# An attention block with a gated Mish branch on one core: two kinds of VectorE step may be planned onto GpSimd, and the planner's thresholds are set anew

## The chip, the cores and the metric

The kernel runs on one core of a Trainium2 chip. A core has engines with instruction streams of their own: TensorE (PE) multiplies matrices into PSUM, ScalarE (ACT) applies functions, VectorE (DVE) and GpSimd (POOL) do elementwise work, and SyncE (SP) issues most transfers. Engines wait for one another through semaphores. The metric is the device time of one execution in microseconds; the median of three runs of the kernel before is 791.36 us (791.05 to 792.82).

## The reference, cut to what matters

`x` has 2,048 tokens of 640 features. A gate per token mixes multi-head attention (32 heads of 20 features) with a dense layer under Mish.

```python
x = A_x
g = _sigmoid((x * gate_w).sum(-1, keepdims=True))
# a: softmax attention
qkv = (x @ wqkv).reshape(B, S, 3, H, Dh)...          # H = 32, Dh = 20
p = softmax(einsum("bhqd,bhkd->bhqk", q, k) * Dh ** -0.5)
a = einsum("bhqk,bhkd->bhqd", p, v)... @ wo
# b: h = x @ w1 + b1 (1,536 wide); Mish: h * tanh(softplus(h)); then @ w2
b = einsum("bsf,fd->bsd", h * jnp.tanh(sp), w2)
return g * a + (1 - g) * b
```

All inputs and the output are bfloat16.

## The kernel before, in words

**Tiles and steps.** Queries are cut into four blocks `c` of 512, keys into 16 tiles `kt` of 128, and the 32 heads into eight groups `g` of four. A score tile (128 keys by 512 queries of one head) fills one PSUM bank. There are 4 x 8 x 16 x 4 = 2,048 of them, taken three at a time: 683 steps. `emit_s` issues a step's score matmuls (L1197) two steps ahead into banks 0 to 2 or 3 to 5, and `emit_e` the exponential (L1219) from there into a ring ETS of six. `emit_pv` and `pv` multiply the exponentials with V (L1456) into bank 6, for four heads at once. V has a column of ones in front of each head, so the sums of the softmax arise beside the products.

**VectorE's share of the exponentials.** In some steps ScalarE takes two tiles and VectorE the third. `choose` decides on that, step by step. `emit_x` evicts such a tile with a scale and a bias to int16 (L1264), so that its bits read as a rough power of two. When four tiles of a group are together, `close` lists three SBUF steps for them: `fraction` (L1328), `times_y` (L1332) and `power` (L1336). Their results enter the product with V as two terms.

**After a group** of four heads and 512 queries, `group_done` copies bank 6 to OUNG (L1538). A transfer brings the sums to RR, `invert` takes reciprocals (L1545) and sends them to DRAM (L1546), four transfers spread them to BCT (L1552), and `times` (L1506) multiplies OUNG by BCT into the normalised tile. The last group of the last block is cut in two halves of 256 queries; these are turned by VectorE itself (L1523 to L1531), the first half through OUNG.

**The dense branch.** `h_task` computes h, and VectorE adds the bias (L953). For every four 128-row pieces ScalarE makes a tanh (L976) into U, and `mish` lists eight VectorE steps: the first rounds U to half precision (L998, from float32), the others are a polynomial (L998, L1001) and the product with h (L1001). `b_task` multiplies with W2 (L1017, evicted at L1024), `p_task` projects the heads and mixes with the gate (L1041, L1047); `part_task` does the same early for the last block, without the last two groups.

**What sets the order.** A planner in Python writes all five instruction streams out when the kernel is built. `Plan.add` keeps a planned clock for each engine from costs such as WIDE (0.60 us) and TAIL. VectorE's listed SBUF steps wait in lanes: `norm` (reciprocals and products), `soon` (the chains of `close`), `blend` (Mish) and `bg`. The function `dve` puts an eviction on VectorE after `work` has filled the time before it with listed steps that fit. TensorE's other matmuls are tasks with due steps, and `pick`, `put` and the main loop place them into bank 7 (`FB`). `choose` refuses a tile when VectorE owes too much (`BEHIND`, `IDLE`), when a group's chain would end late (`tight`, with `CROWD`), or when tasks lag (`LAG`, `room`). GpSimd has the opening's fills and copies and one addition at the very end (L1864).

Of the kernel before, what the change touches and what calls it, by code (L numbers as in the profile page):

```python
# [37 lines left out]
OLD = 3  # L38
WAITED = 3
OWE = 0.2  # L40
# [15 lines left out]
STREAM = 0.5  # L56
# [3 lines left out]
QUICK = 0.335  # L60
FAST = 0.335
# [18 lines left out]
AHEAD = 14  # L80
SPREAD = 3
GAP = 0.3
SLOW_LOAD = 5.0
# [5 lines left out]
CROWD = 1.4  # L89
MARGIN = 2.5  # L90
EAGER = 20
# [5 lines left out]
SHIFT = 0.2  # L97
LAG = 5
SPARE = 7
WINDOW = 3.41  # L100
CALM = 3
# [4 lines left out]
SQ = 24  # L106
SQ_STEP = 16
H_AT = 150
H_STEP = 12.5
# [3 lines left out]
CUTS = ((0, 256), (256, 256))  # L113
# [17 lines left out]
WARM = 7  # L131
MORE = 8
# [11 lines left out]
class Plan:  # L144
# [3 lines left out]
    def __init__(self, prefix):  # L148
        self.prefix = prefix
        self.ops = []  # L150
        self.now = {e: 0.0 for e in ENGINES}
        self.kind = None
        self.passes = deque()
        self.queue = 0.0

    def add(self, eng, fn, deps=(), slot=None, cost=0.1, kind="F", tail=None, bulk=0.0):
# [12 lines left out]
        if eng == "pe":  # L169
            self.passes.append((at + cost, cost))  # L170
        op.t1 = at + cost + (tail or (TAIL["sp"] if slot else TAIL[eng]))
# [71 lines left out]
def bass_gated_mix__softmax_full_mha__dense_activation_mish__prompt_kernel(  # L243
# [142 lines left out]
    def attention(pl, fast):  # L386
# [10 lines left out]
        now = {"step": -1, "open": None, "bank": False, "rate": 9.0}  # L397
# [45 lines left out]
        def dve(fn, deps=(), cost=0.1, kind="F"):  # L443
# [3 lines left out]
            return pl.add("dve", fn, deps, cost=cost, kind=kind)  # L447
# [5 lines left out]
        def work(until):  # L453
            while True:
                best = None
                lined = sorted([lane for lane in (*soon, blend) if lane], key=lambda lane: lane[0][3])
                for rank, todo in enumerate((norm, *lined, bg)):
                    if todo:
# [7 lines left out]
                        halve = len(todo[0]) > 4 and begin + cost > until  # L466
# [53 lines left out]
        if fast:  # L520
# [114 lines left out]
            def fetch(k, g, c, names):  # L635
# [14 lines left out]
                for dst, src in pairs:  # L650
                    op = pl.add("sp", lambda e, dst=dst, src=src: e.dma_start(dst, src), deps, slot, cost=0.5, bulk=1.3 if k else 0.1)  # L651
# [319 lines left out]
            def mish(ev, hb, hc, k):  # L971
# [9 lines left out]
                def piece(cost, fn, after=None):  # L981
                    def run():
                        last[0] = pl.add("dve", fn, [last[0]], cost=cost)
                        if after:
                            after(last[0])
                    blend.append((cost, run, lambda: last[0], due))
# [16 lines left out]
                piece(WIDE, scalar(W, U, 1.0), read)  # L1003
                piece(QUICK, scalar(B, W, MISH_IN))
                piece(WIDE, times(B, W, B))
                piece(QUICK, scalar(B, B, MISH_MID))
                piece(WIDE, times(B, B, B))
                piece(QUICK, scalar(B, B, MISH_BY, MISH_BY * MISH_OUT))
# [264 lines left out]
        def dve_by(fn, deps, cost, slack):  # L1273
# [3 lines left out]
            return pl.add("dve", fn, deps, cost=cost)  # L1277

        def close(batch):
# [15 lines left out]
            def piece(cost, fns, deps, after=None, split=False):  # L1295

                def run(some, each, mark):
                    def go():
                        for sp in some:
                            op = pl.add("dve", fns(sp), deps(), cost=each)  # L1300
# [696 lines left out]
```

## Time and profile before

| | before |
|---|---|
| median of three runs | 791.36 us |
| profiled execution | 791.27 us |
| its span, first to last instruction | 789.4 us |
| busy, ScalarE | 773.3 us (98%) |
| busy, VectorE | 748.6 us (95%) |
| busy, TensorE | 709.7 us (90%) |
| busy, GpSimd | 20.2 us (3%) |
| exponentials on three tiles / on two | 281 / 402 |

A row of the groups gives line, engine, operation, output<-input with shapes, count, busy time and mean duration of one in ns, and the idle time ahead of it with what ended it. Instructions of one engine overlap by a little, so the distance from one start to the next is shorter than a duration. A row of waits reads: who waited for whom, us in total, times, longest. A row of a timeline begins with the start from the span's beginning and the duration, both in us.

### The profile page before, as it was taken

The page shows a single profiled execution, that of the slowest core. Times are in us where ns is not written, and L with a number is a line of the kernel's source. Part 1 is how long each engine was busy: PE and PEld are TensorE (multiplying, and loading weights), DVE is VectorE, ACT ScalarE, POOL GpSimd, SP SyncE. Part 2 cuts the span into 40 slices and gives each one's busy share as a digit, 9 for nine tenths or more (in the row PEclk, how much of TensorE's full clock was granted, in tenths as well). Part 3 has the DMA queues.
Part 4 walks back from the last instruction along what each step waited for, and adds up shares of the span by engine and source line. Part 5 has one row for each costly group of instructions (what it writes and reads, how often), then busy time and mean ns, then how long its engine had stood idle before and what let it go on. Part 6 is the DMA issues. An engine that isn't in the chain of part 4 may idle for free.

```text
span 789.4 us, 16424 instructions
## 1 busy us (share of the span) xinstructions
PE 709.7 (90%) x6649; PEld 262.4 (33%) x6690; DVE 748.6 (95%) x1313; ACT 773.3 (98%) x715; POOL 20.2 (3%) x21
## 2 busy tenths in 40 slices
PE   8899999889888888999999889999889899999985
PEld 4333333233323332233323233333333333333332
DVE  5899999999999999999999999999999999999995
ACT  6999999999999999999999999999999999999995
POOL 8100000000000000000000000000000000000000
PEclk9999999999999999999999999999999999999998
DMA  8221310212233221402112131202121213000101
GB/s 201 63 59 55 102 52 17 81 55 60 72 91 109 83 64 45 133 17 65 32 29 51 52 90 36 64 19 61 31 85 49 82 48 85 15 28 24 29 15 39
DMA packets 77799, 47.12 MB, mean 60 GB/s; under 512 B 23916, under 2 KB 73700, under 8 KB 77668
## 3 DMA queue, kind: packets, MB, share of 16 engines
q1 hardware_dynamic: 77316, 45.80, 21.0%
q8 instruction: 56, 0.92, 0.5%
q14 instruction: 27, 0.22, 0.1%
q10 hardware_dynamic: 288, 0.16, 0.1%
q0 software_dynamic: 112, 0.01, 0.1%
HBM read 36.26 MB, written 7.52 MB: 55 GB/s over the span
## 4 chain that ended last, share of the span: by engine, by line
ACT 90%; DVE 4%; PE 4%; DMA 1%; issue 0%; SPq 0%
ACT ETS L1219 87%; ACT REG L976 2%; PE PS L1197 1%; PE PS L1456 1%; ACT W2R L976 1%; DVE KT L1332 1%; DVE KT L1264 1%; DMA QT<-QS 1%; PE PS L555 0%; DVE QT L1264 0%; PE PS L1041 0%; SPq L651 0%; PE PS L738 0%; DVE HB L1047 0%; DVE HB L1264 0%
## 5 line engine op out<-in xcount | busy, mean ns | idle before, releaser
L1219 ACT ACTIVATE ETS<-PS 128x1024 bf16<-128x1024 f32 (+1 forms) x683 | 753.9, 1370 | 2.8 <-PE PS L1197 2.8
L1197 PE MATMUL PS<-QT,KT 32*128 32x512 bf16 (+1 forms) x2116 | 267.8, 378 | 57.1 <-ACT ETS L1219 48.1
L1456 PE MATMUL PS<-ETS,V_all 128*21 128x512 bf16 (+1 forms) x1699 | 161.7, 375 | 0.0
L1197 PEld LDWEIGHTS PS<-QT,KT 32*128 32x128 bf16 x2116 | 67.0, 91 | 281.6 <-ACT ETS L1219 255.9
L1264 DVE TENSOR_SCALAR PADS<-PS 128x512 int16<-128x512 f32 x97 | 66.0, 682 | 7.8 <-PE PS L1197 7.3
L1264 DVE TENSOR_SCALAR QT<-PS 128x512 int16<-128x512 f32 x102 | 69.5, 683 | 4.0 <-PE PS L1197 3.4
L1017 PE MATMUL PS<-W2R,HB 128*128 128x320 bf16 x384 | 68.5, 302 | 0.7 <-DVE HB L953 0.5
L1264 DVE TENSOR_SCALAR OTN<-PS 128x512 int16<-128x512 f32 x84 | 57.1, 681 | 0.6 <-PE PS L1197 0.5
L943 PE MATMUL PS<-XB,REG 128*128 128x256 bf16 x360 | 53.6, 274 | 2.3 <-DVE OUTT L1047 1.4
L1456 PEld LDWEIGHTS PS<-ETS,V_all 128*21 128x21 bf16 x1699 | 41.8, 90 | 41.4 <-issue 27.0
L1001 DVE TENSOR_TENSOR U<-U 128x1024 f16<-128x1024 f16 x72 | 49.0, 681 | 0.3
L1017 PEld LDWEIGHTS PS<-W2R,HB 128*128 128x128 bf16 x384 | 30.7, 97 | 32.4 <-issue 19.7
L943 PEld LDWEIGHTS PS<-XB,REG 128*128 128x128 bf16 x360 | 29.1, 97 | 25.8 <-issue 23.5
L953 DVE TENSOR_TENSOR HB<-PS,B1T 128x512 bf16<-128x512 f32 x48 | 32.7, 680 | 0.5 <-PE PS L943 0.3
L998 DVE TENSOR_SCALAR U<-U 128x1024 f16<-128x1024 f16 x72 | 29.9, 415 | 0.5
L1041 PE MATMUL PS<-WOQ,QT 128*128 128x320 bf16 x128 | 24.5, 302 | 2.3 <-DVE HB L1047 0.6
L1264 DVE TENSOR_SCALAR REG<-PS 128x512 int16<-128x512 f32 x38 | 25.7, 682 | 0.2
L1735 PE MATMUL PS<-KT 128*128 128x512 bf16 x79 | 24.1, 383 | 1.7 <-issue 1.1
L1041 PE MATMUL PS<-WOQ,OTN 128*128 128x320 bf16 x128 | 23.8, 302 | 0.2 <-issue 0.2
L815 PE MATMUL PS<-REG,XB 128*128 128x160 bf16 (+1 forms) x240 | 23.1, 234 | 0.0
L976 ACT ACTIVATE REG<-HB 128x1024 f32<-128x1024 bf16 x18 | 22.2, 1236 | 0.0
L660 PE MATMUL PS<-XB,REG 128*128 128x512 bf16 x69 | 20.3, 382 | 1.8 <-issue 1.1
(188 smaller groups left out, 816.0 us busy)
## 6 DMA issues: line engine op xcount, KB each, us to landing
REG<-in_B_w_dram SPq DMA_DIRECT2D x36, 320.0 KB, 3.2
BCT<-SUMS SPq DMA_DIRECT2D x124, 64.0 KB, 2.2
W2R<-in_B_w_dram SPq DMA_DIRECT2D x12, 320.0 KB, 3.8
KT<-KS SPq DMA_DIRECT2D x28, 128.0 KB
QT<-QS SPq DMA_DIRECT2D x112, 20.0 KB
QS<-WOQ SPq DMA_DIRECT2D x16, 128.0 KB, 1.7
KS<-OTN SPq DMA_DIRECT2D x16, 128.0 KB, 1.7
W2R<-in_B_w_dram SPq DMA_DIRECT2D x1, 1920.0 KB, 10.2
```

The lines of the kernel that those rows point to most:

```text
L943: return lambda e, bank: e.matmul(PS[:, bank, i * HW:(i + 1) * HW], w1b(n1)[:, f, i * P:(i + 1) * P], xt(c)[:, f, cols], start=(f == 0), s ...
L953: ev = dve(lambda e: e.tensor_tensor(hb, PS[:, bank, :].rearrange("p (i t) -> p i t", i=2), bias, ALU.add), [last, b_load, *guarded, *b_re ...
L976: ex = pl.add("act", lambda e: e.activation(U, h, AF.Tanh, scale=0.5, bias=-MISH_AT), [ev, u_free[0]], cost=0.95)
L998: return lambda e: e.tensor_scalar(dst, src, *ops)
L1001: return lambda e: e.tensor_tensor(dst, one, two, ALU.mult)
L1017: return lambda e, bank: e.matmul(PS[:, bank, 0:HALF], HB[:, hc % 2, f, t * P:(t + 1) * P], W2[:, f, half * HALF:(half + 1) * HALF], start ...
L1041: return lambda e, bank: e.matmul(PS[:, bank, 0:HALF], otn(c, g, fast)[:, t * P:(t + 1) * P], WOG[:, g, half * HALF:(half + 1) * HALF], st ...
L1197: op = pl.add("pe", lambda e, i=i, g=real(g), tile=tile, j=j, cols=cols, c=c, of_q=of_q: e.matmul(scores(s)[:, i, cols], KT[32 * j:32 * j ...
L1219: e_op[s] = pl.add("act", lambda e: e.activation(ETS[:, s % NETS, 0:n, :], scores(s)[:, 0:n, :], AF.Exp, scale=SCALE, bias=LIFT if fast el ...
L1264: ev = dve_by(lambda e: e.tensor_scalar(block(batch["y"], n, I16), scores(s)[:, 2, :], SCALE * ULPS, BIAS, ALU.mult, ALU.add), [s_op[s], * ...
L1456: lasts[n] = pl.add("pe", lambda e, v=v, j=j, src=src[:, cols], of_q=of_q, count=count: e.matmul(PS[32 * j:32 * j + EW, ACC, of_q], v, src ...
L1735: pl.add("pe", lambda e: e.matmul(PS[:, bank, :], k[:, 0:P], k, start=True, stop=True), [free], cost=PASS, kind="S")
```

## The change

Five things are changed.

- **GpSimd takes steps.** A normalising product and Mish's first step are listed with a job for GpSimd. After each eviction on VectorE, a new function `settle` looks at the row of planned instructions at the end of VectorE's line that are not SBUF steps (these have kind "L"). If the job (1.35 us for a product, 1.05 us for a first step, and 0.1 more) fits beside that row, it goes to GpSimd, behind the instruction that begins the row. `patient` holds such a step back from VectorE for 4 us of VectorE's time after its input is there, except in the last 60 steps. Afterwards either engine may get it.
- **The last two halves** work in U2 in place of OUNG, BCT and RR, and no longer bring the listed products ahead of them.
- **After the last step** tasks take banks 7, 5 and 4 in turn.
- **Order and due steps:** the partial projections are due 36 steps ahead of the end (26 before), the first projections of the last block 12 ahead (2 before); the first queries' pads, the estimate's matmuls and Mish's tasks have other due steps.
- **Thresholds** of `choose` and of the main loop have other values, steps that may move are counted at 0.3 of their cost, and a list NUDGE of 86 values, one for eight steps, is taken from the lateness that `choose` sees.

```diff
-OLD = 3
+OLD = 2
-OWE = 0.2
+OWE = 0.6
-STREAM = 0.5
+STREAM = 0.48
+ASIDE = 1.35
+ASIDE_1 = 1.05
+APART = 0.1
+AWAIT = 4
+SHARE = 0.3
+AWAIT_1 = 0
+CALM_END = 60
-RISK = {"pe": 0.1, "act": 0.3, "dve": 0.5, "pool": 1.2, "sp": 0.6}
-CHAIN = 2.6
+RISK = {"pe": 0.1, "act": 0.3, "dve": 0.5, "pool": 0.3, "sp": 0.6}
+CHAIN = 3.0
-IDLE = 5
+IDLE = 7
-AHEAD = 14
-SPREAD = 3
+AHEAD = 20
+SPREAD = 4
-SLOW_LOAD = 5.0
+SLOW_LOAD = 3.5
-CROWD = 1.4
+CROWD = 1.1
-EAGER = 20
+EAGER = 45
-SHIFT = 0.2
-LAG = 5
+SHIFT = 0.4
+LAG = 25
-CALM = 3
+CALM = 2
-SQ = 24
+SQ = 40
-H_STEP = 12.5
+H_STEP = 14
+DIRECT = 1
+PART_DUE = 36
+LAST_DUE = 12
+FETCH = (2.3, 3.0)
+LEAD = 10
+NUDGE = [-0.5, 0, -0.5, 0, -0.5, 0, 0, 0, -0.5, 0, -0.5, 0, 0, -1, 0.5, 0, 0, 1, 0, 0, -1, -1, 2, 2, 1, 0, 0, 0.5, 0, 0, 0, 0, 2, 3, 0, 0, 0, -1, 0.5, 3, 0, 1, -1, 0.5, 0, 0, 0, 0, 1, 0, 0, 0, 0, 3, 0, -1, 0, 0.5, 1, 1, 2, 2, 2, 3, 0, -1, -0.5, 0, 0, 3, -0.5, -0.5, 3, 0.5, 1, 1, 0, 0.5, 0, 2, -0.5, 0.5, 0.5, 0, 0, 3]
...
+        def settle():
+
+            while fast:
+                for todo in (blend, norm):
+                    job = todo[0][5] if todo and len(todo[0]) > 5 else None
+                    ready = job and job[0]()
+                    if not ready:
+                        continue
+                    line = pl.line
+                    i = len(line)
+                    while i and not line[i - 1][2]:
+                        i -= 1
+                    begin = max(ready.t1 + HOP, pl.now["pool"], line[i - 1][0])
+                    while i < len(line) and line[i][0] <= begin:
+                        i += 1
+                    if begin + job[1] + APART <= pl.now["dve"]:
+                        todo.popleft()
+                        job[2](line[i - 1][1])
+                        break
+                else:
+                    return
+
+        def patient(op, wait):
+
+            return now["step"] < NSLOT - CALM_END and pl.now["dve"] < op.t1 + wait
+
+        def load(job):
+
+            return job[0] * (SHARE if len(job) > 5 else 1)
...
-                piece(WIDE, scalar(W, U, 1.0), read)
+                piece(WIDE, scalar(W, U, 1.0), read, AWAIT)
...
-            late = max(0.0, pl.now["dve"] - pl.now["act"])
-            urgent, other = (sum(t[0] for todo in some for t in todo) for some in ((norm, *soon), (blend, bg)))
+            late = max(0.0, pl.now["dve"] - pl.now["act"]) - NUDGE[s // 8]
+            urgent, other = (sum(load(t) for todo in some for t in todo) for some in ((norm, *soon), (blend, bg)))
...
             if end:
-                while norm:
-                    norm.popleft()[1]()
+                if not fast:
+                    while norm:
+                        norm.popleft()[1]()
...
+                    free = [bc_read[0], rr_read[0], oung_free[0]]
+                    if fast:
+                        bc, rr, free = U2[:, CW:CW + w], U2[:, CW + HW:CW + HW + w // 32], [None] * 3
                     cost = w * COL * 2.6 + 0.09
                     if (c, g) != groups[-1]:
-                        held = OUNG[:, cols]
+                        held = U2[:, 0:w] if fast else OUNG[:, cols]
...
+            if fast and c == NC - 1 and g >= NG - DIRECT:
...
-                norm.append((WIDE, lambda: times(src, wide), lambda: wide[-1]))
+                norm.append((WIDE, lambda: times(src, wide), lambda: False if fast and patient(wide[-1], AWAIT) else wide[-1],
+                             0, None, (lambda: wide[-1], ASIDE, lambda dep: times(src, [*wide, dep], "pool"))))
...
-            parts = [part_task(t, half, NSLOT - 26) for t in range(4) for half in range(2)]
-            parts += [p_task(NC - 1, t, half, NSLOT - 2, True) for t in range(last_t[0]) for half in range(2)]
+            parts = [part_task(t, half, NSLOT - PART_DUE) for t in range(4) for half in range(2)]
+            parts += [p_task(NC - 1, t, half, NSLOT - (LAST_DUE, LAST_DUE, 2)[t], True) for t in range(last_t[0]) for half in range(2)]
...
+        def spot():
+
+            if not fast or now["step"] < NSLOT:
+                return FB
+            bank = (FB, 5, 4)[now["spot"] % 3]
...
```

The branch behind `DIRECT` normalises a group of the last block with VectorE's own transposes in place of transfers.

More of the change, by code (lines that the diff above doesn't have):

```diff
@@ L396, in attention @@
         acts = deque()
-        now = {"step": -1, "open": None, "bank": False, "rate": 9.0}
+        spots = {FB}
+        now = {"step": -1, "spot": 0, "open": None, "bank": False, "rate": 9.0}
         if fast:
@@ L979, in mish, with piece, run @@
                 due = ex.t1 + PATIENCE
-                def piece(cost, fn, after=None):
-                    def run():
-                        last[0] = pl.add("dve", fn, [last[0]], cost=cost)
+                def piece(cost, fn, after=None, wait=0):
+                    def run(eng="dve", *more):
+                        last[0] = pl.add(eng, fn, [last[0], *more], cost=ASIDE_1 if more else cost, kind="L")
                         if after:
                             after(last[0])
-                    blend.append((cost, run, lambda: last[0], due))
+                    dep = lambda: False if wait and patient(last[0], wait) else last[0]
+                    job = (lambda: last[0], ASIDE_1, lambda op: run("pool", op))
+                    blend.append((cost, run, dep, due, None, job) if wait else (cost, run, dep, due))
                 def read(op):
@@ L1369, in tight @@
                 left = ends / TAKEN * EXP
-                before = sum(t[0] for t in blend if t[3] < pl.now["act"] + left)
+                before = sum(load(t) for t in blend if t[3] < pl.now["act"] + left)
                 return (late + urgent + before) * CROWD + need + MARGIN >= left
@@ L1714, in backlog @@
         def backlog():
-            return max(0.0, pl.now["dve"] - pl.now["act"]) + sum(t[0] for todo in (norm, *soon, blend, bg) for t in todo)
+            return max(0.0, pl.now["dve"] - pl.now["act"]) + sum(load(t) for todo in (norm, *soon, blend, bg) for t in todo)
         def pv_ready():
```

68 lines of the change are left out of this document (48 added, 20 removed).

## The prediction

> **What bounds the kernel now.** I read the page's first part, then a table of stages, then ScalarE's waits, then the groups of instructions with shapes kept apart, and last the timeline of VectorE. The stages are: before the first softmax exponential, the first 100 us, the long middle, the last exponentials, and the tail. Behind each engine stand its busy us and, in brackets, its instructions.
>
> ```profile
> span 789.4 us, 16424 instructions
> PE 709.7 (90%) x6649; PEld 262.4 (33%) x6690; DVE 748.6 (95%) x1313; ACT 773.3 (98%) x715; POOL 20.2 (3%) x21
> ```
>
> ```profile
> core 0: us, PE busy (x) PEld busy (x) DVE busy (x) ACT busy (x) POOL busy (x), PEclk, DMA share, GB/s
> 0.00:9.28 9.28, 7.60 (x48) 4.74 (x48) 5.01 (x12) 3.31 (x7) 6.31 (x11) 1.00 0.85 182
> 9.28:100.00 90.72, 81.79 (x878) 32.39 (x887) 78.79 (x138) 89.72 (x83) 13.07 (x10) 1.00 0.32 86
> 100.00:764.00 664.00, 604.32 (x5492) 218.12 (x5518) 649.16 (x1135) 663.22 (x613) 0.00 (x0) 1.00 0.20 55
> 764.00:780.60 16.60, 13.80 (x226) 6.18 (x228) 12.02 (x23) 16.53 (x14) 0.00 (x0) 1.00 0.09 23
> 780.60:789.40 8.80, 2.18 (x18) 1.00 (x17) 3.62 (x9) 0.53 (x1) 0.86 (x1) 0.75 0.26 74
> ```
>
> ```profile
> ACT ETS L1219 <- PE PS L1197: 2.8, 6, 1.0
> ```
>
> From 9.28 to 780.60 us ScalarE is busy for 769.47 of 771.32 us, and it waits for scores only 2.8 us in all. So the time is a head of 9.28 us, ScalarE's work, and a tail of 8.80 us. The profiled execution is 791.27 us around a span of 789.4 us, and is 0.09 us under the median of 791.36; I sum against 791.27.
>
> ScalarE's work is no constant, since VectorE takes a share of the exponentials:
>
> ```profile
> L1219 ACT ACTIVATE ETS<-PS 128x1536 bf16<-128x1536 f32 x281 | 446.8, 1621 | 2.2 <-PE PS L1197 2.2
> L1219 ACT ACTIVATE ETS<-PS 128x1024 bf16<-128x1024 f32 x402 | 441.4, 1195 | 0.6 <-PE PS L1197 0.6
> ```
>
> In 402 of the 683 steps ScalarE exponentiates two score tiles in place of three, and the third is VectorE's. Such a tile saves ScalarE 1.621 - 1.195 = 0.426 us. What it costs VectorE is read off start to start, because neighbours overlap by some 0.08 us:
>
> ```profile
> 330.60 0.68 DVE L1328 TENSOR_SCALAR PADS<-QT 128x2048 int16<-128x2048 int16 x1
> 331.20 0.68 DVE L1264 TENSOR_SCALAR QT<-PS 128x512 int16<-128x512 f32 x1
> 331.80 1.21 DVE L1332 TENSOR_TENSOR PADS<-PADS,QT 128x2048 f16<-128x2048 f16 x1
> 332.93 0.68 DVE L1264 TENSOR_SCALAR QT<-PS 128x512 int16<-128x512 f32 x1
> 333.53 0.68 DVE L1336 TENSOR_SCALAR QT<-QT 128x2048 int16<-128x2048 int16 x1
> 334.13 1.39 DVE L1264 TENSOR_SCALAR REG<-PS 128x512 int16<-128x512 f32 x2
> ```
>
> One eviction (L1264) takes 0.60 us, and the three SBUF steps that serve four tiles take 0.60 + 1.13 + 0.60 = 2.33 us. A tile therefore costs 0.60 + 2.33/4 = 1.18 us of VectorE. VectorE is busy 649.16 of 664.00 us in the middle, so it is full too: the two engines are in balance. If VectorE is relieved of w us, it spends them on tiles until both end together again, and the end moves by d with d = 0.426 (w - d)/1.18. That gives **d = 0.265 w**. This exchange rate prices every part below: a microsecond off VectorE is worth about a quarter.
>
> **The change part by part.** *What may move to GpSimd.* Two kinds of VectorE instruction: the normalising product and Mish's first step.
>
> ```profile
> L1506 DVE TENSOR_TENSOR OTN<-OUNG,BCT 128x512 bf16<-128x512 f32 x16 | 10.9, 682 | 0.0
> L1506 DVE TENSOR_TENSOR QT<-OUNG,BCT 128x512 bf16<-128x512 f32 x15 | 10.2, 680 | 0.0
> L998 DVE TENSOR_SCALAR U<-REG 128x1024 f16<-128x1024 f32 x18 | 12.3, 683 | 0.0
> L998 DVE TENSOR_SCALAR U<-W2R 128x1024 f16<-128x1024 f32 x6 | 4.0, 674 | 0.0
> 316.43 0.68 DVE L1506 TENSOR_TENSOR OTN<-OUNG,BCT 128x512 bf16<-128x512 f32 x1
> 317.03 0.68 DVE L1001 TENSOR_TENSOR HB<-U,HB 128x1024 bf16<-128x1024 f16 x1
> ```
>
> These are 16 + 15 products and 18 + 6 first steps, 55 in all, at 0.60 us start to start (316.43 to 317.03). So w lies between 0 and 33 us, and the gain between 0 and 8.7 us.
>
> *How many find a place.* A job goes only where planned VectorE instructions that are not SBUF steps stand in a row for 1.45 us (product) or 1.15 us (first step). The planner waits 4 us for such a row after the job's input is there. In the timeline from 322 to 327 us one row long enough for either is to be seen:
>
> ```profile
> 322.74 0.68 DVE L1336 TENSOR_SCALAR QT<-QT 128x2048 int16<-128x2048 int16 x1
> 323.95 0.69 DVE L1264 TENSOR_SCALAR QT<-PS 128x512 int16<-128x512 f32 x1 [0.53 <-PE PS L1197]
> 324.56 0.68 DVE L1538 COPY OUNG<-PS 128x512 f32<-128x512 f32 x1
> 326.21 0.69 DVE L1264 TENSOR_SCALAR QT<-PS 128x512 int16<-128x512 f32 x1 [0.97 <-PE PS L1197]
> 326.94 0.69 DVE L1328 TENSOR_SCALAR REG<-QT 128x2048 int16<-128x2048 int16 x1
> ```
>
> Between the SBUF steps at 322.74 and 326.94 stand three evictions and 3.5 us. The pair at 334.13 is a short row: 1.39 us, enough for a first step alone. Two rows of one kind and the other within some 12 us make a first step find a place within its 4 us a little over half the time, and a product a little less. The wait helps, since a held first step also holds back the seven SBUF steps behind it. I take 28 of 55, an estimate from these two rows: w = 28 x 0.60 = 16.8 us, **-4.5 us**. The ends, 0 and 55 jobs, are kept for the range.
>
> *What GpSimd needs for them.* Its prices are not in the trace at these sizes. The nearest rows:
>
> ```profile
> 25.18 0.21 POOL L591 COPY REG<-OUTT 128x5 bf16<-128x5 bf16 x1 [3.04 <-DMA OUTT<-in_gate_w_dram]
> 5.78 0.52 POOL L577 COPY WOQ<-WOQ 128x400 bf16<-128x400 bf16 x1 [1.99 <-DMA WOQ<-in_A_wqkv_dram]
> 783.66 0.86 POOL L1864 TENSOR_TENSOR HB<-PADS,W2R 128x320 bf16<-128x320 f32 x1 [758.27 <-ACT PADS L1862]
> 783.65 1.00 DVE L1047 SCALAR_TENSOR_TENSOR HB<-PS,GATE,W2R 128x320 bf16<-128x320 f32 x2
> ```
>
> A two-input step on 320 columns takes 0.86 us. On 512 it takes 0.21 + 0.65 x 1.6 = 1.25 us if 0.21 us is fixed, and 1.38 us if all of it scales; the planner's 1.35 lies between. A copy of 400 columns takes 0.52 us, so 1,024 take 1.00 to 1.33 us against the planner's 1.05. GpSimd has nothing else from 100 us on, so this time is hidden. What is exposed is an overrun: where the job ends later than planned, the next SBUF step may be held. From -0.10 to +0.28 us a job, I take 0.10 over 28 jobs: 2.8 us of VectorE, **+0.7 us**. Behind a late first step wait Mish's second step on VectorE and, through the buffer U, the next tanh; behind a late product, the next group's copy of the sums into OUNG. Products come one group, some 25 us (771.32/31), apart, so that last wait costs nothing while the 4 us stay below this.
>
> *The thresholds, the order and the nudges.* Higher limits (7 in place of 5 us of VectorE work after one taken tile, 25 in place of 5 steps of lag, a factor 1.1 in place of 1.4 on a group's remaining work, moved jobs counted at 0.3) let VectorE take tiles that it now refuses. They work on its idle time: 11.93 us in the first stage of exponentials, 14.84 us in the middle and 4.58 us in the last, together 31.35 us. Part of that is in gaps such as the 0.53 and 0.97 us above, which no limit fills. From 0 to 20 us, I take 12: **-3.2 us**. Below nothing is possible as well, if a fuller VectorE answers late; that is a rival.
>
> *The halves in U2.* They no longer share OUNG, BCT and RR with the last full group, so its product need not come first:
>
> ```profile
> 772.13 0.68 DVE L1506 TENSOR_TENSOR QT<-OUNG,BCT 128x512 bf16<-128x512 f32 x1
> 772.92 0.42 DVE L1523 COPY OUNG<-PS 128x256 f32<-128x256 f32 x1
> ```
>
> All this lies 8 us ahead of the last exponential, on an engine with 4.58 idle us there, and the tail behind that exponential keeps its instructions. I price this at nothing, from -0.5 to +0.5 us. The same holds for the projections due earlier (12 and 36 steps ahead of the end), for three PSUM banks in turn after the last step, and for fetches planned at 2.3 and 3.0 us. Their cover is TensorE's 664.00 - 604.32 = 59.68 us of slack in the middle. The direct normalisation under DIRECT costs nothing: with 1 it asks for g of at least 7 in the last block, and those groups are the halves, which return earlier. No DMA is added or moved.
>
> Sum: 791.27 - 4.5 + 0.7 - 3.2 = **784.3 us**, 0.9% below; the 0.09 us to the median is smaller than anything here.
>
> **The rivals.** *The larger gain.* 50 jobs move and 22 us of idle time fill: 52 x 0.265 = 13.8, **777.5 us**. For it speaks that held jobs make room themselves; against it, that the pair at 334.13 is too short for a product.
>
> *It does not do what it says.* Few rows are found at the right moment and the limits only shift tiles in time: 5 jobs, 0.8 us, **790.6 us**. For it speaks that in the rows from 330.60 to 334.13 evictions stand singly.
>
> *Slower, by a block between the two engines.* If VectorE stands still while GpSimd works, a product costs it 1.35 in place of 0.60 us and a first step 1.05 in place of 0.60: for all 55, 31 x 0.75 + 24 x 0.45 = 34 us, +9.0, **800 us**. It decides from 0.60 us of standstill per job on. Against it:
>
> ```profile
> 6.95 12.28 POOL L584 MEMSET QT<- 128x2048 bf16 x7
> 15.25 0.69 DVE L1264 TENSOR_SCALAR PADS<-PS 128x512 int16<-128x512 f32 x1 [0.82 <-PE PS L1197]
> ```
>
> The eviction at 15.25 runs beside GpSimd's memset and takes its usual 0.69 us, and the two sums at 783.65 take 0.50 us each beside the addition at 783.66. For it: no row shows a GpSimd read of SBUF beside an SBUF step.
>
> The Trainium skill, "SBUF — State Buffer", section "Who interferes with whom", says that VectorE and GpSimd share one pair of ports under an exclusive lock. A VectorE instruction in a two-port mode, or with two SBUF inputs against a GpSimd read, blocks for the whole other instruction, while one with at most one SBUF input outside those modes does not. The two rows agree on the free case; the block itself no row here shows. By that rule the evictions are safe and only overruns into an SBUF step cost, so the sum stays; if plan and chip drift apart by a whole job, it gives the 800 us. "Perfetto Trace Analysis", section "Optimizing Scalar/DVE Operations", also of the Trainium skill, warns that offloading between these two might not help.
>
> *Slower, by a late VectorE.* With more tiles admitted the chains end late, the sums behind them are held, and ScalarE waits. Its 2.8 us of waits would have to grow by more than the 7 us of gain; at 12 us, 791.3 - 7 + 9.2 = **793.5 us**.
>
> **How the numbers follow.** The forecast (780 to 788.5) has 0.62; the larger gain 0.15; no effect 0.09; the block 0.08; the late VectorE 0.06. This kernel's runs can tell 0.2%, 1.6 us, from no change. Faster: 0.62 + 0.15 + 0.05 of the no-effect case = 0.82; the same: 0.04; slower: 0.14. The range runs from 777 to 791.5: it leaves out half of the larger gain and the two slower cases.
>
> **What would show it.** After the change POOL should count about 49 instructions in place of 21, L1506 and L998 about 28 fewer on VectorE, the 128x1024 exponentials about 419 in place of 402, ScalarE's stretch about 764 us, head and tail as now. L1264 stays at 0.68 us if evictions are not blocked; L1328, L1332 and L1336 keep their 0.60 and 1.13 us. The prediction is wrong if the 1,024 count does not rise, if ScalarE's waits grow by several us, or if SBUF steps stretch beside GpSimd.

## The result and the profile after

The changed kernel takes 794.98 us, the kernel before 792.01 us beside it (medians of nine runs each). The ratio is 1.0038, with a 95% interval from 1.0028 to 1.0048. It is 0.4% slower, where 0.9% faster was forecast. One of the changed kernel's nine runs took 1,283.87 us, far from the other eight (794.03 to 797.64 us), and is not in the ratio. The profiled execution is 795.01 us around a span of 793.1 us, 3.7 us longer than before's 789.4 us.

The first part of the page after, with span, instructions, and each engine's busy us, share and instructions:

```profile
span 793.1 us, 16569 instructions
PE 717.4 (90%) x6693; PEld 264.6 (33%) x6693; DVE 751.0 (95%) x1330; ACT 769.4 (97%) x715; POOL 80.2 (10%) x49
```

GpSimd has its 28 jobs: 49 instructions in place of 21. But it is busy 60.0 us more than before, which is 2.14 us a job. The groups of instructions with shapes kept apart (count, then busy us and mean ns of one, then the engine's idle time ahead) say which job is the long one:

```profile
L1050 POOL TENSOR_SCALAR U<-REG 128x1024 f16<-128x1024 f32 x12 | 33.2, 2770 | 240.2 <-ACT ETS L1271 100.4 <-DVE PADS L1386 42.6 <-DVE REG L1386 27.4
L1050 POOL TENSOR_SCALAR U<-W2R 128x1024 f16<-128x1024 f32 x4 | 11.1, 2772 | 83.8 <-DVE OTN L1560 34.5 <-DVE QT L1390 20.4 <-DVE HB L1382 19.9
L1560 POOL TENSOR_TENSOR OTN<-OUNG,BCT 128x512 bf16<-128x512 f32 x8 | 10.1, 1267 | 258.1 <-DVE W2R L1390 66.2 <-DVE HB L1390 49.8 <-DVE QT L1386 39.2
L1271 ACT ACTIVATE ETS<-PS 128x1024 bf16<-128x1024 f32 x418 | 429.1, 1125 | 4.3 <-PE PS L1249 3.9
L1271 ACT ACTIVATE ETS<-PS 128x1536 bf16<-128x1536 f32 x265 | 399.2, 1534 | 4.3 <-PE PS L1249 3.5
```

The product, 1.27 us, is the one that was planned at 1.35. Mish's first step takes 2.77 us, where 1.05 was planned. The last two rows show that VectorE did take over tiles: 418 exponentials of two tiles, where before had 402. Yet ScalarE ends later. The waits of the same trace (us in total, times, longest):

```profile
DVE U L1050 <- POOL U L1050: 9.9, 13, 1.5
ACT ETS L1271 <- PE PS L1249: 7.3, 14, 1.5
PE PS L1249 <- DVE QT L1316: 4.6, 6, 1.5
PE PS L1249 <- DVE OTN L1316: 2.7, 5, 0.9
```

VectorE now waits 9.9 us for GpSimd's first steps, score matmuls wait for VectorE's evictions, and ScalarE's wait for scores has grown from 2.8 to 7.3 us. Once ScalarE's tanh also waits 1.1 us for GpSimd itself, for the buffer that the first step reads. How one is handed to the next is to be seen at 305 us (the timeline: start, us, engine, line; in brackets the idle time ahead and what ended it):

```profile
305.23 2.77 POOL L1050 TENSOR_SCALAR U<-W2R 128x1024 f16<-128x1024 f32 x1 [8.94 <-DVE REG L1386]
306.29 0.68 DVE L1390 TENSOR_SCALAR QT<-QT 128x2048 int16<-128x2048 int16 x1
308.03 0.43 DVE L1050 TENSOR_SCALAR U<-U 128x1024 f16<-128x1024 f16 x1 [1.07 <-POOL U L1050]
309.10 0.68 DVE L1316 TENSOR_SCALAR QT<-PS 128x512 int16<-128x512 f32 x1
309.93 0.39 PE L1249 MATMUL PS<-QT,KT 32*128 32x512 bf16 x3 [0.53 <-DVE QT L1316]
310.37 1.45 ACT L1271 ACTIVATE ETS<-PS 128x1536 bf16<-128x1536 f32 x1 [0.34 <-PE PS L1249]
```

GpSimd ends at 308.00, VectorE's next Mish step starts at 308.03 after 1.07 idle us, the eviction that stands two steps behind it starts at 309.10, the score matmul had waited 0.53 us for that bank, and the exponential 0.34 us for the scores.

One measure serves for all the kernels below. I call **stretch** the time from the first exponential to the end of the last. **Work** is what ScalarE would need for it without disturbance: 1.331 us for a three-tile exponential, 0.904 us for a two-tile one and 0.947 us for each of the 24 tanh steps. These are the median distances between neighbouring starts in the trace of before. **Loss** is stretch minus work. All in us:

| | stretch | two-tile exponentials | work | loss | tail |
|---|---|---|---|---|---|
| before | 771.25 | 402 | 760.1 | 11.1 | 8.85 |
| after | 774.36 | 418 | 753.3 | 21.0 | 9.39 |

So the change did take 6.8 us of work from ScalarE, and it brought 9.9 us of new loss. The tail adds 0.5 us and the head 0.1 us, which makes the 3.7 us of the span. The recorded waits don't make up the whole of the loss: before loses 11.1 us with only 2.8 us of waits for scores. The question is what causes the loss.

### The profile page after: what moved, and what is told of

Its sections match the earlier page's. It is cut to its first block, busy times and chain, and to the rows that moved or that the text cites. A ratio compares the mean times of both kernels' runs of the same rounds, so it can differ in the third digit from the quotient of the medians.

```text
span 793.1 us, 16569 instructions
## 1 busy us (share of the span) xinstructions
PE 717.4 (90%) x6693; PEld 264.6 (33%) x6693; DVE 751.0 (95%) x1330; ACT 769.4 (97%) x715; POOL 80.2 (10%) x49
## 4 chain that ended last, share of the span: by engine, by line
ACT 56%; DVE 28%; PE 10%; POOL 4%; issue 1%; POOLq 0%; DVEq 0%
ACT ETS L1271 55%; POOL U L1050 4%; DVE U L1053 3%; PE PS L1249 3%; PE PS L1510 3%; DVE QT L1316 3%; DVE U L1050 2%; DVE OTN L1316 2%; DVE HB L1003 2%; DVE PADS L1316 1%; DVE REG L1316 1%; DVE QT L1386 1%; DVE PADS L1386 1%; DVE HB L1053 1%; PE PS L1093 1%
## 5 line engine op out<-in xcount | busy, mean ns | idle before, releaser
L1510 PE MATMUL PS<-ETS,V_all 128*21 128x512 bf16 (+1 forms) x1680 | 165.3, 378 | 0.4 <-DVE OUNG L1599 0.4
L1316 DVE TENSOR_SCALAR QT<-PS 128x512 int16<-128x512 f32 x111 | 75.2, 681 | 2.5 <-PE PS L1249 2.3
L1316 DVE TENSOR_SCALAR OTN<-PS 128x512 int16<-128x512 f32 x91 | 61.0, 677 | 0.1
L1050 POOL TENSOR_SCALAR U<-REG 128x1024 f16<-128x1024 f32 x12 | 33.2, 2770 | 240.2 <-ACT ETS L1271 100.4
L1316 DVE TENSOR_SCALAR PADS<-PS 128x512 int16<-128x512 f32 x68 | 46.3, 682 | 2.5 <-PE PS L1249 2.3
L1316 DVE TENSOR_SCALAR REG<-PS 128x512 int16<-128x512 f32 x54 | 36.4, 678 | 0.4 <-PE PS L1249 0.3
L1560 POOL TENSOR_TENSOR OTN<-OUNG,BCT 128x512 bf16<-128x512 f32 x8 | 10.1, 1267 | 258.1 <-DVE W2R L1390 66.2
L1316 DVE TENSOR_SCALAR KT<-PS 128x512 int16<-128x512 f32 x42 | 28.7, 682 | 1.9 <-PE PS L1249 1.9
```

The costliest lines, as they stand in the source:

```text
L1050: return lambda e: e.tensor_scalar(dst, src, *ops)
L1316: ev = dve_by(lambda e: e.tensor_scalar(block(batch["y"], n, I16), scores(s)[:, 2, :], SCALE * ULPS, BIAS, ALU.mult, ALU.add), [s_op[s], * ...
L1510: lasts[n] = pl.add("pe", lambda e, v=v, j=j, src=src[:, cols], of_q=of_q, count=count: e.matmul(PS[32 * j:32 * j + EW, ACC, of_q], v, src ...
```

## The experiments

Three theories stood against each other. **The price:** the first step is dear on GpSimd by itself, the order was planned for 1.05 us, and VectorE stands behind it. **The block:** the two engines get in each other's way in SBUF, and GpSimd's steps are slow or VectorE's stand still because of that. **The order:** the new limits and nudges admit tiles whose chains (the three SBUF steps behind four of VectorE's tiles) end late, and GpSimd has little to do with it. I first held that the price is nearly the whole of it, and that the kernel gets faster as soon as the dear steps are taken away.

**Products alone.** Mish's first step may no longer move:

```diff
-                piece(WIDE, scalar(W, U, 1.0), read, AWAIT)
+                piece(WIDE, scalar(W, U, 1.0), read)
```

> The changed kernel, but Mish's first step stays on VectorE; products may still go to GpSimd (8 do in this plan). Theory M (Mish's first step takes 2.77 us on GpSimd where 1.05 was planned, VectorE stands behind it and evictions come late): VectorE waits for GpSimd 0 us, ScalarE's stalls fall from about 18 us back to about 8, time 787 to 789, 0.5% under before. Rival T (the looser thresholds fill VectorE until its evictions come late): 794 or more, stalls as in the changed kernel. Rival P (the products on GpSimd block VectorE's SBUF steps): 792 to 794.

**The true price in the plan.** The planner counts 2.8 us and looks for rows of that length:

```diff
-ASIDE_1 = 1.05
+ASIDE_1 = 2.8
```

> The changed kernel with one number other: the planned GpSimd time of Mish's first step 2.8 us in place of 1.05. One such step and 9 products then still go to GpSimd. Theory M: as with products alone, 787 to 789, VectorE's waits for GpSimd under 1 us. Rival T: 794 or more.

**No jobs.** The edit of products alone, and this:

```diff
-                norm.append((WIDE, lambda: times(src, wide), lambda: False if fast and patient(wide[-1], AWAIT) else wide[-1],
-                             0, None, (lambda: wide[-1], ASIDE, lambda dep: times(src, [*wide, dep], "pool"))))
+                norm.append((WIDE, lambda: times(src, wide), lambda: wide[-1]))
```

> The changed kernel with neither kind of step given to GpSimd and none held back; thresholds, order, nudges and the halves in U2 stay. Theory M: 788 to 790.5, some 1.3 us (8 products x 0.60 x 0.265) over the products alone, and faster than before by the thresholds' part. Rival T: 793 to 797. Rival P: faster than the products alone.

**The prices by themselves.** In the kernel before, after GpSimd's small copy near 25 us, each candidate step runs twice in a chain on GpSimd alone (F is 1,024 columns of float32, H of float16, low of bfloat16, high.bitcast(FP32) the same place as float32):

```diff
+            probe = [pl.add("pool", lambda e: e.memset(F, 0.5), cost=1.0)]
+            price(lambda e: e.tensor_scalar(H, F, 1.0, None, ALU.add))
+            price(lambda e: e.tensor_copy(H, F))
+            price(lambda e: e.tensor_tensor(H, F, F, ALU.add))
+            price(lambda e: e.tensor_scalar(high.bitcast(FP32), F, 1.0, None, ALU.add))
+            price(lambda e: e.tensor_scalar(H[:, 0:CW], F[:, 0:CW], 1.0, None, ALU.add))
+            price(lambda e: e.tensor_scalar(H, H, 1.0, None, ALU.add))
+            price(lambda e: e.tensor_tensor(low[:, 0:CW], F[:, 0:CW], F[:, CW:2 * CW], ALU.mult))
```

> The kernel before with 14 more GpSimd instructions near 25 to 60 us, where GpSimd is idle, each kind twice: float32 to half precision by tensor_scalar on 1,024 columns, the same by tensor_copy and by tensor_tensor, tensor_scalar float32 to float32, on 512 columns, from half precision, and the product on 512. Theory M: the disputed tensor_scalar takes 2.7 to 2.8 us here too, so that it is the instruction's own price. Rival (it is drawn out by VectorE's evictions beside it): 1.0 to 1.4 us where VectorE does nothing beside it and more elsewhere. The product takes 1.27 us. The kernel's time stays within 1% of before.

Measured, with the ratio to before and its 95% interval:

| | us | ratio | jobs on GpSimd | stretch | two-tile | work | loss | tail |
|---|---|---|---|---|---|---|---|---|
| products alone | 799.95 | 1.0099 (1.0080 to 1.0117) | 11 products | 776.8 | 414 | 755.0 | 21.8 | 11.9 |
| true price | 801.38 | 1.0119 (1.0102 to 1.0137) | 12 products, 1 first step | 776.85 | 411 | 756.3 | 20.6 | 12.9 |
| no jobs | 798.89 | 1.0086 (1.0070 to 1.0103) | 0 | 775.15 | 414 | 755.0 | 20.1 | 12.55 |

All three are slower than the changed kernel, the one without any job too. My theory as I had stated it fell: taking the dear step away costs time when the planner makes a new order from the same limits. The price run, on the other hand, bears out its first half. Its timeline of GpSimd, each row two steps:

```profile
26.84 5.67 POOL L601 TENSOR_SCALAR HB<-U 128x1024 f16<-128x1024 f32 x2
32.58 2.40 POOL L602 CAST HB<-U 128x1024 f16<-128x1024 f32 x2
35.06 3.86 POOL L603 TENSOR_TENSOR HB<-U 128x1024 f16<-128x1024 f32 x2
39.02 6.00 POOL L604 TENSOR_SCALAR HB<-U 128x1024 f32<-128x1024 f32 x2
45.10 3.37 POOL L605 TENSOR_SCALAR HB<-U 128x512 f16<-128x512 f32 x2
54.76 2.61 POOL L607 TENSOR_TENSOR HB<-U 128x512 bf16<-128x512 f32 x2
```

Adding a constant to 1,024 columns takes 2.8 us here as it does in the changed kernel. Copies of the same tile take 1.30 and 1.04 us, the first beside a VectorE step that begins with it, and a sum of the tile with itself takes 1.9 us. The price is the instruction's own. It doesn't come from a neighbour: five of the changed kernel's 16 first steps ran beside no SBUF step of VectorE, and they took 2.77 us like the others. It doesn't come from a narrow result either: with a float32 result the step takes 2.77 and 3.15 us. (This kernel's single time, 796.68 us, has the flags' transfer waiting behind the probe, so it says nothing.)

A part of why the kernel without jobs is so slow is in its waits and in the timeline of its end:

```profile
ACT ETS L1271 <- PE PS L1510: 8.1, 6, 2.7
ACT PADS L1949 <- PE PS L1093: 5.6, 1, 5.6
```

```profile
785.02 0.62 DVE L1382 TENSOR_SCALAR OTN<-REG 128x1024 int16<-128x1024 int16 x2
785.67 1.03 DVE L1386 TENSOR_TENSOR OTN<-OTN,REG 128x1024 f16<-128x1024 f16 x2
786.76 0.40 PE L1510 MATMUL PS<-OTN,V_all 128*21 128x256 f16 x6 [2.24 <-DVE OTN L1386]
```

ScalarE waits for PV matmuls, up to 2.7 us at a time, and those wait for VectorE's late chains. The last exponential ends at 784.51. After it VectorE still works on the chain of its last tiles, PV waits for that, and the tail has 12.55 us in place of 8.85. That is the order's doing, with no GpSimd in it.

So each comparison so far changed two things, the steps and the order. The next run changes the step alone.

**The same order, with a copy.** Where the step runs on GpSimd it copies; the order of every engine's instructions is that of the changed kernel. The 1 that the step adds is left out in those 16 steps:

```diff
+                        what = (lambda e: e.tensor_copy(W, U)) if more else fn
-                        last[0] = pl.add(eng, fn, [last[0], *more], cost=ASIDE_1 if more else cost, kind="L")
+                        last[0] = pl.add(eng, what, [last[0], *more], cost=ASIDE_1 if more else cost, kind="L")
```

> The changed kernel with every instruction in its place and the same order on each engine; only where Mish's first step is on GpSimd, it is a tensor_copy to half precision (1.20 us in the price run) in place of the tensor_scalar (2.77 us). This leaves out the added 1, so Mish's result differs for those 16 steps. Theory M (the step's true duration costs the changed kernel its gain): VectorE's waits for GpSimd fall from 9.9 us to under 1, ScalarE's lost time from 21 us to 12, and the time to 786 to 788, below before. Rival T (the thresholds, in this very order, are too tight for the chip): 792 or more.

Measured: 786.3 us, ratio 0.9932 (0.9909 to 0.9956), 8.7 us less than the changed kernel. The groups, the wait for scores, and the middle of the table of stages (us, then busy us with instructions of PE, PE's loads, VectorE, ScalarE and GpSimd, clock, DMA share, GB/s):

```profile
L1033 POOL CAST U<-REG 128x1024 f16<-128x1024 f32 x12 | 12.5, 1041 | 253.2 <-ACT ETS L1272 93.0 <-DVE PADS L1387 44.3 <-DVE OTN L1391 24.1
L1272 ACT ACTIVATE ETS<-PS 128x1024 bf16<-128x1024 f32 x418 | 437.7, 1158 | 1.1 <-PE PS L1250 1.1
```

```profile
ACT ETS L1272 <- PE PS L1250: 3.0, 7, 1.0
```

```profile
100.00:764.00 664.00, 605.69 (x5557) 220.79 (x5583) 650.78 (x1150) 662.32 (x617) 29.32 (x26) 1.00 0.20 55
```

The same row of the changed kernel:

```profile
100.00:764.00 664.00, 604.77 (x5453) 217.15 (x5453) 642.07 (x1131) 655.87 (x609) 56.99 (x26) 0.99 0.20 55
```

With 1.04 us a step, VectorE is busy 8.7 us more of the same 664 us, ScalarE 6.5 us more, no wait of VectorE for GpSimd is left among the waits, and the loss falls from 21.0 to 12.0 us. That settles the price as the cause within this order: 16 steps that are 1.73 us longer than in this run cost 8.7 us.

**The parts alone, under the limits of before.** Three more runs look at what else the change does. The first keeps the jobs and the holding back, with the true price, and sets every limit back; the second is the kernel without jobs with the nudges at zero; the third has neither jobs nor limits nor nudges, so that the halves in U2 and the banks after the last step remain (and RISK's entry for GpSimd, which the first and third don't set back):

All three have `NUDGE = [0] * 86`, the second and third also the edit of no jobs. The first and third set the limits back, among them those below; the first has the last line too:

```diff
-IDLE = 7
+IDLE = 5
-AHEAD = 20
+AHEAD = 14
-CROWD = 1.1
+CROWD = 1.4
...
-LAG = 25
+LAG = 5
...
-ASIDE_1 = 1.05
+ASIDE_1 = 2.8
```

> The GpSimd part with the kernel before's thresholds, order and no nudges, Mish's step planned at 2.8 us: 10 products and one first step go to GpSimd, the halves use U2. By the relief alone (11 x 0.60 x 0.265) 789.5 to 791. But the plan shows 396 exponentials on two tiles where before has 402: if the holding back costs VectorE its order, ScalarE's work grows by 6 x 0.426 = 2.6 us and the time is 793 to 795.

> No step on GpSimd, the new thresholds and order, but all 86 nudges zero. The plan has 405 exponentials on two tiles (before 402, with nudges 414). If the nudges make the tail of 12.6 us and the late chains of the run without jobs: 790 to 793, tail under 10 us. If the thresholds make them: 796 or more.

> No step on GpSimd, the kernel before's thresholds, order and due steps, no nudges: what is left is the halves in U2, without the listed products ahead of them, and the three banks after the last step. 403 exponentials on two tiles. Predicted at nothing, from -0.5 to +0.5 us: 791.5 to 792.8, tail 8.5 to 9.3 us.

| | us | ratio | stretch | two-tile | work | loss | tail |
|---|---|---|---|---|---|---|---|
| jobs (10 products, 1 first step), limits of before | 802.29 | 1.0131 (1.0109 to 1.0153) | 775.58 | 395 | 763.1 | 12.4 | 14.9 |
| limits without jobs and nudges | 795.09 | 1.0047 (1.0029 to 1.0066) | 771.94 | 404 | 759.3 | 12.6 | 11.7 |
| halves in U2 and banks alone | 792.38 | 1.0001 (0.9991 to 1.0012) | 772.87 | 402 | 760.1 | 12.7 | 8.8 |

The halves and the banks cost nothing and bring nothing, as forecast. The limits alone bring two more tiles and a tail 2.8 us longer; their 795.09 us lies between the two forecasts, so neither the nudges nor the limits account for the whole of the trouble. Against the run without jobs, the nudges account for 10 of its 12 extra tiles and for 7.5 us of its 20.1 us of loss. The nudges belong to one order, and in another they do harm. The first row is a miss (793 to 795 us was the highest forecast) that I can't explain fully: with 11 jobs VectorE took fewer tiles, and the chain of the last batch ended late: of its 10.7 us more span, 3.0 us are ScalarE's work on those tiles and 6.1 us the tail. Why the planner refuses tiles there stays open.

**The same order, with a sum.** The step does the full computation again: GpSimd adds a tile of ones, a single column read over and over, with the two-input instruction that took 1.9 us in the price run. The order is the changed kernel's, with one memset more on GpSimd:

```diff
+    ONE = sb("ONE", [P, 1], FP32)
+                        what = times(W, U, ONE[:, 0:1].to_broadcast([P, 2 * CW]), ALU.add) if more else fn
```

> The changed kernel in the same order, with Mish's first step on GpSimd done as a tensor_tensor sum of U and a column of ones spread over 1,024 columns: the full computation, 1.93 us by the price run, between the copy (1.04 us) and the tensor_scalar (2.77 us). If the loss goes with the step's duration in a straight line, ScalarE loses 12.0 + 9.0 x 0.89/1.73 = 16.6 us and the time is 790 to 791.5; if it grows only with what goes beyond a slack of half a microsecond or so, 788 to 790.

Measured: 789.71 us, ratio 0.9972 (0.9961 to 0.9984), loss 16.1 us, near the 16.6 of the straight line. In one and the same order the first step of 1.04, 1.89 and 2.77 us gives a loss of 12.0, 16.1 and 21.0 us, and a time of 786.3, 789.7 and 795.0 us. But the trace shows that the middle one loses its time in another way. Here is the place that was shown at 305 us, first with the sum, then with the copy:

```profile
303.07 1.89 POOL L1056 TENSOR_TENSOR U<-W2R,ONE 128x1024 f16<-128x1024 f32 x1 [8.93 <-DVE REG L1389]
304.15 1.36 DVE L1393 TENSOR_SCALAR QT<-QT 128x2048 int16<-128x2048 int16 x1
305.44 0.41 DVE L1053 TENSOR_SCALAR U<-U 128x1024 f16<-128x1024 f16 x1
```

```profile
301.90 1.04 POOL L1033 CAST U<-W2R 128x1024 f16<-128x1024 f32 x1 [8.92 <-DVE REG L1387]
302.98 0.68 DVE L1391 TENSOR_SCALAR QT<-QT 128x2048 int16<-128x2048 int16 x1
303.58 0.42 DVE L1051 TENSOR_SCALAR U<-U 128x1024 f16<-128x1024 f16 x1
```

From the chain step to Mish's second step VectorE needs 0.60 us beside the copy, 1.29 us beside the sum and 1.74 us beside the added constant. Beside the added constant the chain step keeps its 0.68 us and VectorE then waits for the result. Beside the sum the chain step itself lasts 1.36 us, until 305.51, 0.55 us after GpSimd ends at 304.96, and the wait is gone. So the block is real, but it depends on GpSimd's instruction, and on when VectorE's step begins (see the last section). From 160 to 700 us of this run 12 of VectorE's SBUF steps are stretched so, 11 of them beside sums, by 6.7 us in all against their median durations.

**A new order at the true price, and its control.** The sum of the last run with its price in the plan, and limits and nudges chosen anew for it; and the same without any job, limits and nudges again chosen anew:

With jobs, beside the sum above:

```diff
-ASIDE_1 = 1.05
+ASIDE_1 = 1.95
-AWAIT = 4
+AWAIT = 6
-EAGER = 45
+EAGER = 30
-LAG = 25
+LAG = 10
-LAST_DUE = 12
+LAST_DUE = 2
...
```

Without jobs, beside the edit of no jobs:

```diff
-IDLE = 7
+IDLE = 5
-LAG = 25
+LAG = 10
-LAST_DUE = 12
+LAST_DUE = 8
...
```

> The same sum on GpSimd, planned at its own 1.95 us, and thresholds and nudges chosen anew by the planner for this price: 19 products and a few first steps go to GpSimd, 415 exponentials on two tiles. Work 268 x 1.331 + 415 x 0.904 + 22.7 = 754.6 us; with a loss of 11 to 13 us, as in the kernel before and in the same-order copy, head 9.4 and tail 9 to 10: 786 to 789, faster than before. If a new order is the chip's trouble and not the price, 793 or more.

> No step on GpSimd, thresholds and nudges chosen anew by the planner for that: 413 exponentials on two tiles. Work 755.4 us; with a loss of 11 to 13: 787 to 790. If GpSimd's relief is what makes the gain, it is not under 790; if the thresholds and nudges make most of it, it lies within 2 us of the run with the sum.

| | us | ratio | jobs | stretch | two-tile | work | loss | tail |
|---|---|---|---|---|---|---|---|---|
| with jobs | 784.92 | 0.9909 (0.9892 to 0.9926) | 19 products, 2 first steps | 765.29 | 414 | 755.0 | 10.3 | 8.2 |
| without | 786.92 | 0.9936 (0.9920 to 0.9953) | 0 | 766.75 | 412 | 755.9 | 10.9 | 8.9 |

The first of them is faster than both kernels of this case. Its page, its exponentials and its wait for scores:

```profile
span 783.1 us, 16589 instructions
PE 713.6 (91%) x6676; PEld 264.9 (34%) x6717; DVE 749.4 (96%) x1336; ACT 768.3 (98%) x715; POOL 48.1 (6%) x43
```

```profile
L1274 ACT ACTIVATE ETS<-PS 128x1024 bf16<-128x1024 f32 x414 | 443.6, 1185 | 0.2 <-PE PS L1252 0.2
L1563 POOL TENSOR_TENSOR OTN<-OUNG,BCT 128x512 bf16<-128x512 f32 x11 | 13.9, 1268 | 348.6 <-DVE PADS L1393 91.9 <-DVE QT L1393 86.2 <-DVE KT L1385 47.1
```

```profile
ACT ETS L1274 <- PE PS L1252: 1.5, 3, 1.0
```

Fewer tiles than the changed kernel, 414 for 418, but half its loss. The plan moves 19 products at 1.27 us, which it had priced rightly, and only 2 first steps. Of the 7.1 us against before, an order made anew brings 5.1 us without GpSimd, and the kernel with 21 jobs is 2.0 us faster still. The times of the two lie apart (784.62 to 784.94 against 786.78 to 787.16 us), so this difference is real. That the jobs make it is not shown: limits and nudges differ too, and each kernel is one order out of many that the planner could make.

## Why the prediction was wrong, point by point

**The bound was right, but its sum had no term for the loss.** Head, ScalarE's work, the loss and the tail make the time in every run. The forecast took 7.0 us from ScalarE's work, and 6.8 us went. What it put at nothing is new loss: 9.9 us came, and 9.0 of them go with the copy. ScalarE is busy 655.87 of 664 us in the changed kernel's middle and 662.32 us with the copy.

**The exchange rate was right on ScalarE's side and is not borne out on VectorE's.** A tile fewer saves 0.427 us of ScalarE by the distances between starts (0.426 was taken). That relieved time turns into tiles, one for 1.18 us, is not what the last pair shows. Its 21 jobs free 21 x 0.60 = 12.6 us, which should give 8 tiles and 3.3 us. The kernel with jobs has 2 tiles more; VectorE is busy 749.4 us in place of 758.0, and the 2.0 us are 0.9 of work, 0.6 of loss and 0.7 of tail, less 0.2 of head.

**The number of jobs was right, to the unit by luck.** The forecast took 28 of 55 from two rows of a timeline, and 12 products and 16 first steps moved. Two of its signs came out, 49 instructions on GpSimd (49 named) and 418 two-tile exponentials (419 named). The 418 is right as a sum only: the run without any job has 414, so the jobs can't be shown to bring the 10 or so that the exchange rate gives for them. ScalarE's stretch, 764 us by the forecast, came to 774.36.

**The step that failed is "What GpSimd needs for them".** It priced the first step from GpSimd's copy of 400 columns at 1.00 to 1.33 us, an overrun of at most 0.28 us a job, taken at 0.10 us. A copy does cost that: 1.04 us was measured with the copy. But the first step adds a constant, and that takes 2.77 us. The overrun against the plan is 1.72 us for each of 16 steps, 27.5 us in place of 2.8 us. The row was a copy, and the rate of a copy was taken for the rate of an addition. The two-input row of 0.86 us for 320 columns, scaled to 1,024, would have given 2.3 to 2.8 us; that this holds 2.77 is luck, since the two-input sum of 1,024 columns takes 1.89.

**The conversion of the overrun was near in size and wrong in kind.** The prediction turned it into time at 0.265, as if a lost microsecond of VectorE only meant fewer tiles. It was instead spent as waits inside an order already fixed: the evictions behind it came late, and ScalarE waited for scores. Between the copy and the added constant, 16 x 1.73 = 27.7 us of longer steps cost 8.7 us, about 0.31 of it. By the prediction's 0.265 they would have cost 7.3 us. The main error is the size of the overrun.

**The sum without that error.** The run with the copy has the planned price of 1.05 us and the changed kernel's order in all else. It took 786.3 us against 784.3 forecast: 2.0 us off and inside the range for the likeliest case.

**The thresholds, -3.2 us, were not a term of their own.** Without jobs and nudges the limits cost 0.5%. With nudges and without jobs they cost 0.9%. In neither of these runs do they bring the 3.2 us. The split into -4.5 and -3.2 us has no support in the runs. In the last pair, where each kernel has an order of its own, 5.1 of the 7.1 us come without any job.

**The halves, banks and due times at nothing: right** for the halves and the banks, whose run has a ratio of 1.0001; the due times were never run alone. The tail stayed near 9 us in the changed kernel. It grew to between 11.7 and 14.9 us in the five runs that took away or set back a part of the jobs, limits and nudges and let the planner make a new order from the rest. The prediction called it "as now" and gave no case to that.

**The rivals.** "Late VectorE", with 0.06, came nearest: it named the place (ScalarE waits for scores because VectorE answers late) and gave 793.5 us. Its reason was another, too many tiles admitted. "A block between the two engines" was to decide from 0.60 us of standstill per job on. In the changed kernel VectorE's SBUF steps were stretched by 2.2 us in all beside the 28 jobs, 0.2 us of it beside added constants, so it didn't decide here. Beside the sum it comes to the 6.7 us above.

## What to carry to other kernels

Price a step that is moved to another engine by the same operation on that engine, or measure it alone; a copy of the same tile took 1.04 us where the added constant took 2.77. When an order is written out ahead, a wrong price is paid mostly by what is queued behind the step that reads the result. Limits and nudges that were chosen for one order are not a part of a change that can be kept or left by itself, so compare with a control that has an order of its own, and remember that two orders differ by more than the part in question.

## What the runs showed of the hardware

**GpSimd's added constant is dearer than its sum of two tiles.** On 1,024 columns the constant takes 2.77 us, the sum 1.89 us, the copy 1.04 us, each within a running kernel. In the price run the constant takes 1.49 and 1.80 us on 512 columns, and 2.77 and 3.15 us with a float32 result. The Trainium skill, "GPSIMD Engine Reference", section 4.1, has it the other way: elementwise steps with two inputs are about twice as slow as on VectorE, and those with one input run at roughly line rate. The product agrees, with 1.27 us against VectorE's 0.68. For the added constant the measurement decides against it.

**VectorE's SBUF steps stand still for a part of GpSimd's steps, and the part depends on the instruction.** Beside the sum, VectorE's chain step lasted 1.36 us at 304.15, as shown. In the changed kernel the one long stretch of a large step in the middle stood beside a product, which has two inputs as well:

```profile
460.28 1.27 POOL L1560 TENSOR_TENSOR QT<-OUNG,BCT 128x512 bf16<-128x512 f32 x1
460.34 1.49 DVE L1050 TENSOR_SCALAR U<-U 128x1024 f16<-128x1024 f16 x1 [0.15 <-POOL U L1050]
```

It takes 1.49 in place of 0.43 us and ends 0.28 us after the product. Beside the added constant the start decides. In the changed kernel 14 SBUF steps of VectorE begin 0.94 us or more behind the start of an added constant, and all keep their durations, as the one at 306.29 does. Large steps that begin sooner don't. Here is the one of the changed kernel, and then one of the price run:

```profile
555.75 2.77 POOL L1050 TENSOR_SCALAR U<-REG 128x1024 f16<-128x1024 f32 x1 [81.85 <-ACT ETS L1271]
556.41 1.46 DVE L1386 TENSOR_TENSOR REG<-REG,OTN 128x2048 f16<-128x2048 f16 x1
```

```profile
29.70 2.81 POOL L601 TENSOR_SCALAR HB<-U 128x1024 f16<-128x1024 f32 x1
29.95 1.33 DVE L1348 TENSOR_TENSOR HB<-HB,KT 128x1024 f16<-128x1024 f16 x1
```

They take 1.46 in place of 1.22 us and 1.33 in place of 0.68. Take the usual duration from each end, and VectorE was held until 0.90 us after the constant began, both times. The later part isn't free for every step either: two int16 steps of the price run that begin 1.84 us into a constant take 1.11 in place of 0.28 us.

The Trainium skill, "SBUF — State Buffer", section "Who interferes with whom", describes this as a pair of ports that whoever comes first holds for the whole instruction. The rows beside products and sums agree. The rows beside the added constant, where by that section VectorE's step should have stood still until the end, do not, though the same chain steps do stand still beside the sum. Why that instruction lets VectorE go in between stays open.

**Evictions don't suffer.** The changed kernel's evictions by the tile they write (count, then shortest, median and longest in ns), the largest group of seven:

```profile
L1316 DVE TENSOR_SCALAR QT<-PS x111: 625/681/692, 108.9 to 542.6; 128x512 int16<-128x512 f32 x111
```

In all seven groups, 417 evictions, the longest takes 0.69 us, and in the run with the sum it is the same, whatever GpSimd does beside them. Of VectorE's steps that read PSUM, evictions and others, 48 begin during one of the changed kernel's 28 jobs, and none is stretched.
